# First loads on two queues: queries and keys together on SyncE's, decay table and values on ScalarE's, and eight products of zeros instead of ten

## The chip, the cores and the metric

The kernel runs on one core of a Trainium2 chip. The metric is the device time of one execution in microseconds (us), as the median over several executions. The kernel before takes 665.44 us (median of 6, from 665.19 to 665.92).

## The reference

Two blocks follow each other. The first is a recurrent retention over 4 batches, 8 heads, 768 positions and a head dimension of 64; its output, laid out as 3072 tokens by 512, goes through a two-layer block of width 2048 with a leaky ReLU.

```python
gamma = 1.0 - 2.0 ** (-5.0 - np.arange(H))
scale = 1.0 / np.sqrt(D)
for t in range(S):
    state = gamma[None, :, None, None] * state + einsum('bhd,bhe->bhde', k[:, :, t], v[:, :, t])
    y[:, :, t] = scale * einsum('bhd,bhde->bhe', q[:, :, t], state)
x = y.transpose(0, 2, 1, 3).reshape(3072, 512)
h = x @ w_in                      # 512 x 2048
out = np.maximum(0.01 * h, h) @ w_out   # 2048 x 512
```

## The kernel before

The 768 positions are cut into 6 chunks of 128 (index c), each for 4 batches (b). For one chunk and batch the retention is done in matrix form: `score` multiplies keys by queries (32 small products, L165), `masked` multiplies the result by a triangular mask on VectorE (L187), `decay_v` multiplies the values by a decay per head (L147 on GpSimd, or L151 on ScalarE), `values` multiplies masked scores by values (L210), `reads` adds the part of the running state (L201), `state` and `first_state` form the new state (L225), and `taken` brings the tokens out with their query decay (L255). The tokens of two batches by chunk are then the right-hand side of the two weight layers.

The weights come as 64-bit floats, in 32 pieces of 512 KB. ScalarE (`powers`, L450 to L453) and VectorE (L462, L467, L474) turn each piece into 32-bit floats. The two large layers are done in 2x2 blocks with seven products in place of eight (`seven`, L532); the very first unit alone is done directly (`direct`, L554), in steps that each use one piece.

All this stands in an order written out by hand, and each engine runs its instructions in that order. TensorE's stream at the start is: some products of a cleared tile (`keep_busy`, L744, whose result nobody reads), the scores of chunk 0, batch 0, two small products that spread the decay table over partitions (`tables`, L761 and L763), the scores of batch 1, the `spread` product (L771), the values of batches 0 and 1, the scores of batch 2, one more product of zeros, and then the first step of `direct`.

The first loads are issued from two queues. SyncE's queue (`nc.sync`, SPq in the views) gets queries and keys of batch 0 (512 KB, tile `qk`), values of batch 0 (256 KB, tile `kv`), weight pieces 0 and 1 (tile `raw`), and then queries and keys of batch 2, values of batch 2 and so on. ScalarE's queue (`nc.scalar`, ACTq) gets queries and keys of batch 1, the decay table (24.4 KB, into the tile `rows`, which lies in `t` and is cleared first by GpSimd and VectorE), and values of batch 1. ScalarE then loads its function table and begins to compute only once the decay tables are there. The later loads all come from SyncE's queue; completion semaphores are used in turn, eight of them, so that a later DMA may have to wait for an earlier one's landing.

Of the kernel before, what the change touches and what calls it, by code (L numbers as in the profile page):

```python
# [23 lines left out]
def kernel(  # L24
# [35 lines left out]
    nc = tc.nc  # L60
# [54 lines left out]
    heads = {}  # L115
# [11 lines left out]
            y = flat[:, half : 2 * half].rearrange("p (s h d) -> p s h d", s=2, h=H)  # L127
        heads[c, b] = x, y

    def load_qk(c, b, queue=nc.sync):  # L130
        queue.dma_start(out=heads[c, b][0], in_=qk[c, b])

    def load_v(c, b, queue=nc.sync):
        queue.dma_start(out=heads[c, b][1][:, 1], in_=kv[c, b][:, 1])
# [4 lines left out]
    def load(c, b, place=None):  # L139
        place_for(c, b, place)  # L140
        load_qk(c, b)
        nc.sync.dma_start(out=heads[c, b][1], in_=kv[c, b])
# [15 lines left out]
    def score(c, b):  # L158

        x = heads[c, b][0]  # L160
        ps = scores[c, b] = two_banks(f"ap_{c}_{b}")
        for a in range(HP):
            for u in range(2):
                for j in range(2):
                    nc.tensor.matmul(ps[ts(u, 64), j, a, :], lhsT=x[ts(j, 64), 1, a, ts(u, 64)],  # L165
                                     rhs=x[ts(j, 64), 0, a, :])
# [104 lines left out]
    def ahead(c, b):  # L271


        if c >= NC:
            return
        if b < 2:
            x = work.tile([128, 2, HP, C], FP32, tag="qk", bufs=AHEAD, name=f"qk_{c}_{b}")
        else:
            if b == 2:
                room[c] = new_o(0).rearrange("p i k n -> p (i k n)")  # L280
            x = room[c][:, ds((b - 2) * 2 * HP * C, 2 * HP * C)]
            x = x.rearrange("p (s a t) -> p s a t", s=2, a=HP)
        heads[c, b] = [x, None]
        load_qk(c, b)
# [422 lines left out]
    nothing = t[:, 0, 0, 0:64].bitcast(BF16)  # L707
    half = decay.shape[1] // 2
    load_qk(0, 0)
    load_qk(0, 1, nc.scalar)  # L710
    nc.vector.memset(t[:, 0, 0, 0:64], 0.0)
    nc.gpsimd.memset(rows[:, :half], 0.0)
    nc.vector.memset(rows[:, half:], 0.0)
    nc.scalar.dma_start(out=rows[0:H], in_=decay)
    load_v(0, 0)
    load_v(0, 1, nc.scalar)
    load_piece(0)
    load_piece(1)
# [23 lines left out]
    def keep_busy(n):  # L742
        for _ in range(n):
            nc.tensor.matmul(idle.rearrange("p i (two n) -> p (i two) n", two=2), lhsT=nothing,  # L744
                             rhs=nothing.unsqueeze(1).to_broadcast([128, 4, 128]),
                             start=True, stop=True, skip_group_check=True)
# [9 lines left out]
    def scratch(name, n):  # L756
        return work.tile([128, 2, N], FP32, tag=name, name=f"{name}_x{n}")

    keep_busy(10)
    score(0, 0)  # L760
    nc.tensor.matmul(tables[:, 0, 0:H], lhsT=by_head, rhs=ones, start=True, stop=True,  # L761
                     skip_group_check=True)
# [227 lines left out]
```

## Time and profile before

| what | value |
|---|---|
| median of 6 executions | 665.44 us (665.19 to 665.92) |
| the profiled execution | 665.49 us, of which the span from first to last instruction is 663.4 us |
| mean granted clock of TensorE | 0.999 |
| TensorE busy | 657.6 us (99%) |
| VectorE, ScalarE, GpSimd busy | 371.7, 176.2, 20.5 us |
| TensorE busy in the first 13.7 us | 11.06 us |
| DMA | 48.92 MB in the span; share of the sixteen DMA engines in the first 13.7 us 0.89 |

The profile is that of one execution. Times in its views count from the start of the span. PE is TensorE's products, PEld its loads of the stationary operand, DVE is VectorE, ACT ScalarE, POOL GpSimd, SP SyncE; a line such as "PE ap L165" names the engine, the tile written and the line of the kernel. The chain of waits follows the work back from the last instruction to what released it; a DMA in it stands from its issue to its landing.

### The profile page before, as it was taken

The page shows a single profiled execution, that of the slowest core. Times are in us where ns is not written, and L with a number is a line of the kernel's source. Part 1 is how long each engine was busy: PE and PEld are TensorE (multiplying, and loading weights), DVE is VectorE, ACT ScalarE, POOL GpSimd, SP SyncE. Part 2 cuts the span into 40 slices and gives each one's busy share as a digit, 9 for nine tenths or more (in the row PEclk, how much of TensorE's full clock was granted, in tenths as well). Part 3 has the DMA queues.
Part 4 walks back from the last instruction along what each step waited for, and adds up shares of the span by engine and source line. Part 5 has one row for each costly group of instructions (what it writes and reads, how often), then busy time and mean ns, then how long its engine had stood idle before and what let it go on. Part 6 is the DMA issues. An engine that isn't in the chain of part 4 may idle for free.

```text
span 663.4 us, 10518 instructions
## 1 busy us (share of the span) xinstructions
PE 657.6 (99%) x4537; PEld 574.1 (87%) x4537; DVE 371.7 (56%) x587; ACT 176.2 (27%) x323; POOL 20.5 (3%) x24
## 2 busy tenths in 40 slices
PE   8999999999999999999999999999999999999998
PEld 5888888888888888888888889888888888888886
DVE  5789969889888684243437414527433343431342
ACT  4854555264261002202102211300220210221210
POOL 1000000000000020001001001001000100000000
PEclk9999999999999999999999999999999999999999
DMA  9921422323322650030022003005001001000001
GB/s 339 400 91 33 126 64 77 114 65 107 115 82 77 237 178 1 0 103 26 1 85 107 1 1 127 1 16 176 1 0 33 33 0 48 17 0 1 1 0 63
DMA packets 15757, 48.92 MB, mean 74 GB/s; under 512 B 1752, under 2 KB 2008, under 8 KB 15712
## 3 DMA queue, kind: packets, MB, share of 16 engines
q1 hardware_dynamic: 15408, 47.45, 20.4%
q8 instruction: 35, 0.57, 0.4%
q10 hardware_dynamic: 304, 0.81, 0.3%
q14 instruction: 10, 0.08, 0.0%
HBM read 41.97 MB, written 6.29 MB: 73 GB/s over the span
## 4 chain that ended last, share of the span: by engine, by line
PE 98%; DMA 1%; DVE 0%; issue 0%; DVEq 0%
PE A_o L532 13%; PE B_o L532 13%; PE C_o L532 12%; PE A_h L532 12%; PE B_h L532 12%; PE C_h L532 12%; PE D_o L532 6%; PE D_h L532 6%; PE yp L210 3%; PE d L554 2%; PE ap L301 2%; PE ap L165 2%; PE yp L201 1%; PE sp L225 1%; DMA qk<-in_qk_dram 1%; PE yp L225 0%
## 5 line engine op out<-in xcount | busy, mean ns | idle before, releaser
L532 PE MATMUL A_h<-x,w 128*128 128x256 f32 x368 | 87.7, 381 | 0.0
L532 PEld LDWEIGHTS A_h<-x,w 128*128 128x128 f32 x368 | 69.3, 190 | 9.7 <-issue 0.2
L532 PE MATMUL A_o<-g,w 128*128 128x256 f32 x288 | 68.1, 379 | 0.0
L478 DVE TENSOR_TENSOR m<-m,B_h 128x512 f32<-128x512 f32 x23 | 15.8, 687 | 89.2 <-PE B_h L532 89.2
L532 PEld LDWEIGHTS A_o<-g,w 128*128 128x128 f32 x288 | 54.6, 190 | 7.6 <-issue 0.2
L572 ACT COPY m<-A_h 128x512 f32<-128x512 f32 x23 | 13.5, 585 | 175.8 <-PE A_h L532 155.5
L567 ACT ACTIVATE g<-g 128x512 f32<-128x512 f32 x69 | 42.0, 629 | 66.0 <-DVE g L478 66.0
L478 DVE TENSOR_TENSOR m<-m,B_o 128x512 f32<-128x512 f32 x16 | 11.0, 684 | 64.3 <-PE B_o L532 64.3
L532 PE MATMUL C_h<-t,w 128*128 128x256 f32 x184 | 43.5, 379 | 0.0
L532 PE MATMUL B_h<-x,w 128*128 128x256 f32 x184 | 43.5, 379 | 0.0
L532 PE MATMUL C_h<-x,w 128*128 128x256 f32 x184 | 43.5, 379 | 0.0
L532 PE MATMUL B_h<-t,w 128*128 128x256 f32 x184 | 43.5, 379 | 0.0
L532 PE MATMUL D_h<-t,w 128*128 128x256 f32 x184 | 43.5, 379 | 0.0
L532 PEld LDWEIGHTS C_h<-x,w 128*128 128x128 f32 x184 | 35.0, 190 | 4.8
L532 PEld LDWEIGHTS C_h<-t,w 128*128 128x128 f32 x184 | 35.0, 190 | 4.8
L532 PEld LDWEIGHTS D_h<-t,w 128*128 128x128 f32 x184 | 35.0, 190 | 4.8
L532 PEld LDWEIGHTS B_h<-x,w 128*128 128x128 f32 x184 | 35.0, 190 | 4.8
L532 PEld LDWEIGHTS B_h<-t,w 128*128 128x128 f32 x184 | 35.0, 190 | 4.8
L147 POOL TENSOR_TENSOR kv<-kv,dec 128x512 f32<-128x512 f32 x18 | 19.6, 1089 | 496.5 <-DMA kv<-in_kv_dram 234.8
L481 DVE TENSOR_TENSOR gd<-g,gd 128x512 f32<-128x512 f32 x48 | 33.2, 692 | 1.7
L532 PE MATMUL C_o<-gd,w 128*128 128x256 f32 x144 | 34.0, 379 | 0.0
L532 PE MATMUL B_o<-gd,w 128*128 128x256 f32 x144 | 34.0, 379 | 0.0
(130 smaller groups left out, 1014.8 us busy)
## 6 DMA issues: line engine op xcount, KB each, us to landing
raw<-in_weights_dram SPq DMA_DIRECT2D x31, 512.0 KB, 3.8
kv<-in_kv_dram SPq DMA_DIRECT2D x17, 512.0 KB, 4.8
out_dram<-o SPq DMA_DIRECT2D x23, 256.0 KB, 2.3
qk<-in_qk_dram SPq DMA_DIRECT2D x10, 512.0 KB, 4.5
o<-in_qk_dram SPq DMA_DIRECT2D x8, 512.0 KB, 4.5
in<-in_qk_dram SPq DMA_DIRECT2D x5, 512.0 KB, 8.6
in<-in_kv_dram SPq DMA_DIRECT2D x3, 512.0 KB, 7.8
in<-in_kv_dram SPq DMA_DIRECT2D x4, 256.0 KB, 8.6
```

What stands on the lines that cost most here:

```text
L147: engine.tensor_tensor(out=v, in0=v, in1=gk.unsqueeze(2).to_broadcast([128, H, D]), op=ALU.mult)
L165: nc.tensor.matmul(ps[ts(u, 64), j, a, :], lhsT=x[ts(j, 64), 1, a, ts(u, 64)], rhs=x[ts(j, 64), 0, a, :])
L201: nc.tensor.matmul(ps[ts(i, 64), j, m, :], lhsT=st[b][ts(j, 64), a, :], rhs=x[ts(j, 64), 0, a, :], start=(m == 0), stop=False, skip_group_ ...
L210: nc.tensor.matmul(ps[ts(i, 64), j, m, :], lhsT=y[:, 1, 2 * a + j, :], rhs=am[:, j, a, :], start=(c == 0 and m == 0), stop=True, skip_grou ...
L225: nc.tensor.matmul(sp[ts(j, 64), a, :], lhsT=y[:, 0, 2 * a + j, :], rhs=y[:, 1, 2 * a + j, :], start=start, stop=True, skip_group_check=True)
L301: nc.tensor.matmul(ps[j][ts(u, 64), a, :], lhsT=x[ts(j, 64), 1, a, ts(u, 64)], rhs=x[ts(j, 64), 0, a, :])
L478: nc.vector.tensor_tensor(out=out, in0=a, in1=b, op=ALU.add)
L481: nc.vector.tensor_tensor(out=out, in0=a, in1=b, op=ALU.subtract)
L532: nc.tensor.matmul(half, lhsT=block(w, sa)[:, k, ts(i, 128)], rhs=rhs[:, k, :], start=(first and (i == 0 or split) and n == 0 and k == 0), ...
L554: nc.tensor.matmul(banks[r][:, i, :], lhsT=block(2 * u, r + 2 * kh)[:, k, ts(i, 128)], rhs=x[:, 2 * kh + th, k, :], start=(step == 0 and i ...
L567: nc.scalar.activation(g[:, i], g[:, i], AF.Prelu, alpha=0.01)
L572: nc.scalar.copy(out=got["m1"], in_=ps)
```

## The change

Queries and keys of batches 0 and 1 are both issued from SyncE's queue, one after the other. ScalarE's queue no longer carries queries and keys; it issues the decay table, then the values of batch 0, then those of batch 1. The number of products of zeros at the start goes from ten to eight. All other instructions, their order on each engine and the tiles stay as they are.

```diff
-    def load_qk(c, b, queue=nc.sync):
-        queue.dma_start(out=heads[c, b][0], in_=qk[c, b])
+    def load_qk(c, b):
+        nc.sync.dma_start(out=heads[c, b][0], in_=qk[c, b])
...
     load_qk(0, 0)
-    load_qk(0, 1, nc.scalar)
+    load_qk(0, 1)
     nc.vector.memset(t[:, 0, 0, 0:64], 0.0)
     nc.gpsimd.memset(rows[:, :half], 0.0)
     nc.vector.memset(rows[:, half:], 0.0)
     nc.scalar.dma_start(out=rows[0:H], in_=decay)
-    load_v(0, 0)
+    load_v(0, 0, nc.scalar)
     load_v(0, 1, nc.scalar)
     load_piece(0)
     load_piece(1)
...
-    keep_busy(10)
+    keep_busy(8)
     score(0, 0)
```

## The prediction

> **What bounds the kernel now.** I read the page first, for its shares and the chain that ended last.
>
> ```profile
> PE 657.6 (99%) x4537; PEld 574.1 (87%) x4537; DVE 371.7 (56%) x587; ACT 176.2 (27%) x323; POOL 20.5 (3%) x24
> PE 98%; DMA 1%; DVE 0%; issue 0%; DVEq 0%
> ```
>
> TensorE is busy for 99% of the span and carries 98% of the chain; one per cent of the chain is DMA, at the start. So the change, which touches the first microseconds alone, can only move the moment from which TensorE runs without a gap. The second view is the chain in order of time, cut to the first 30 us (columns: start, duration, what).
>
> ```profile
> 0.80 5.07 DMA qk<-in_qk_dram
> 5.87 0.04 issue
> 5.92 1.10 PE ap L165 x32
> 7.02 0.32 PE tables L761 x2
> 7.34 0.22 PE tables L763 x2
> 7.56 1.03 PE ap L165 x32
> 8.59 1.06 PE spread L771 x2
> 9.65 1.05 PE yp L210 x16
> ...
> 12.60 0.69 DVE w L474
> 13.29 0.04 issue
> 13.33 3.85 PE d L554 x16
> ```
>
> The reader is to see the order: first queries and keys (landed 5.87), scores of batch 0, tables, scores of batch 1, spread, values; then VectorE's work on tokens and on the first weight piece; at 13.33 the first large products. The waits of TensorE after 13 us have a single line, the 0.37 us just ahead of 13.33. What counts is therefore how far 13.33 moves.
>
> The third view is the timeline of the first 5 us (start, duration, engine; SPq and ACTq are the queues of SyncE and ScalarE).
>
> ```profile
> 0.80 0.40 ACTq L131 DMA_DIRECT2D qk<-in_qk_dram  x1
> 0.80 0.38 SPq L131 DMA_DIRECT2D qk<-in_qk_dram  x1
> 1.24 0.42 SPq L134 DMA_DIRECT2D kv<-in_kv_dram  x1
> 1.50 0.52 ACTq L714 DMA_DIRECT2D t<-decay_dram  x1
> 2.05 0.39 ACTq L134 DMA_DIRECT2D kv<-in_kv_dram  x1
> 3.16 0.15 PEld L744 LDWEIGHTS <-t 128*128 128x128 bf16 x1 [0.28 <-issue]
> 3.59 0.61 PEld L744 LDWEIGHTS <-t 128*128 128x128 bf16 x3 [0.28 <-issue]
> ```
>
> The last two lines are the products of zeros: 0.43 us apart until 3.59, then three loads within 0.61 us. The fourth view is the table of stretches (after the stretch: its length, busy time of PE, PEld, DVE, ACT and POOL, then clock, DMA share, GB/s).
>
> ```profile
> 3.00:4.00 1.00, 1.00 (x4) 0.40 (x3) 0.00 (x0) 0.75 (x1) 0.00 (x0) 1.00 0.98 401
> 6.00:8.00 2.00, 2.00 (x56) 1.81 (x60) 0.84 (x1) 0.17 (x1) 0.15 (x1) 1.00 1.03 397
> ```
>
> From 3 us on the sixteen DMA engines are full at about 400 GB/s, so a reordering moves landings against one another, not the total.
>
> **The change part by part.** Everything is set against the profiled execution: span 663.4, time 665.49, so 2.1 us lie around the span; the median 665.44 is 0.05 lower.
>
> *Queries and keys on one queue.* The trace's records of single packets give the price: a 4 KB packet holds an engine 0.159 us, a 2 KB one 0.084; queries and keys of a batch are 8 packets an engine, one batch's values 8 of 2 KB. With both queues filled, their packets alternate. The first packet is slow (0.70 to 1.27 us); on the slowest engine it ends at 3.27. Before, seven more of batch 0 then alternate with six of batch 1 from the other queue: 3.27 + 13 x 0.159 = 5.34, and the landing was at 5.87, some 0.55 later. After, the other queue holds the decay table (one packet of 3 KB, about 0.125) and values: 3.27 + 7 x 0.159 + 0.125 + 5 x 0.084 = 4.93, plus 0.55 gives 5.48. Bounds: 4.93 with nothing between, 5.87 as before. Scores of batch 0 start about 0.4 earlier, near 5.5.
>
> Batch 1 pays for it. Its 8 packets now come after batch 0's, with 8 value packets between: 4.93 + 8 x 0.159 + 8 x 0.084 = 6.87, landing at 7.42, where before it was 6.09 (issued 0.80, landed 5.3 later). Bounds: 6.09, and 7.68 if all the other queue's packets go first (3.27 + 15 x 0.159 + 16 x 0.084 + 0.125 + 0.55). Before, its scores needed it at 7.49 and it had been there for 1.4 us. After, TensorE is ready at about 7.1 (0.4 earlier) and waits for 7.42, so it starts near 7.46: no more than 0.05 us gained. This new wait takes what the old one gave. Queued behind it are spread and values, and VectorE's mask waits for the scores; bounds on this start are 7.1 and 7.72, so -0.4 to +0.25 us.
>
> *Decay table and values.* Decay is issued at 1.50 in both kernels, since it waits for two clearings of its tile that end at 1.40; now it is first on its queue, ahead of 512 KB, and lands near 4 where it was 6.77. The tables need it at about 6.6: no gain, it was there in time. Values of batch 0 are issued at 2.05 instead of 1.24 and land near 5.8 (before 7.09: issue 1.24 and 5.8 to landing), those of batch 1 at 2.45 instead of 2.05 and land near 7.7 (before 9.23: 2.05 and 7.2). GpSimd multiplied batch 1's at 9.30 to 10.34 after a 0.4 us wait; now it starts right behind batch 0's, about 8.9. TensorE needs them at 10.70: this is covered either way, at nothing.
>
> *Queues.* SyncE issues one DMA in place of another, so the weight pieces behind it leave at 1.71 and 2.18 as before. ScalarE still issues three; they end at 2.85 instead of 2.44, and its table load (1.28 us) ends near 4.1. Its first copy starts at 7.60 before, so 3 us of cover hide this. Later issues on SyncE reuse eight completion semaphores in turn: the view of SyncE's waits has 2.5 us for the first DMA. The one behind batch 1's queries moves from 6.26 to about 7.45; its data is wanted by the engines only after 11.4 (batch 2's queries land at 11.37: issued 2.96, 8.4 to landing), and without that cover it would cost up to 1.2 us there.
>
> *Bytes.* Everything that SyncE's queue and the other one carry up to the first weight piece is the same, so this piece still lands at 8.79 (issued 1.71, 7.1 to landing) and the batch 2's queries at 11.37: cost zero, within 0.1 us.
>
> *Two products fewer.* The last two started at 4.10 and 4.32 and nothing but the first scores stands behind them. TensorE stops near 4.3 instead of 4.7, waits till 5.5 instead of 5.9. They cost nothing now, and their absence brings nothing as long as the clock holds, since the data is later.
>
> The sum: -0.05 at the scores of batch 1, 0 elsewhere, carried to 13.33 and the end: 665.49 - 0.05 - 0.05 for the median = 665.4, which I round to 665.35 as the bound on the gain's side is the farther one.
>
> Two rules of the Trainium skill bear on this. The page "DMA: Bandwidth & Descriptors", section "Issuing engines are not separate DMA queues", says that DMAs of all issuing engines interleave on the same sixteen engines and that spreading them saves issue time only; by it alone the change is worth zero. The packets above agree on the sharing, but show that order in a queue moves a landing by 0.4 us or more. The page "TensorE: Matmul & The Clock Gate", section "What's actually happening", speaks against the smaller number of products: the array runs at half rate until about 3.4 us of sustained work; by it eight slow products of 0.427 us, 3.41 us as an estimate, are barely one such stretch.
>
> **The rivals.** *Earlier after all* (0.17): batch 1's data lands before 7.1, for which its packets would need fewer values between them. Then the start moves by 0.4, to 0.6 at most: the batch 2's queries land at 11.37, their scores take 1.03 and the small product behind them 0.2, so 13.33 can't come before 12.7. Time 664.9. For it: the landing of 7.42 is for the slowest engine, whose first packet may be faster another time. Against: the decision needs the last engine.
>
> *Batch 1 late* (0.11): values go through first and 7.68 or later holds. Then +0.25 to +0.5, time 665.8.
>
> *The clock stays low* (0.12), the slower side: place, scores of batch 0 to spread. In the trace the products' pace changed at 3.75, 2.7 us after the first. If in other executions it changes later, ten slow products reach to 1.05 + 4.27 = 5.3 and eight to 4.5, with an idle stretch of a microsecond behind them, and the clock is released only after the scores. Price: twice the time of scores, tables and scores, 1.03 + 0.54 + 1.03 = 2.6 more, less the 0.35 wait for batch 1: about +2.2, time 667.6. It decides (over 1.33 us) when the low clock lasts beyond about 8.8 us in most executions. Against: the six times lie within 0.73 us, and release came while the seventh product ran.
>
> **How the numbers follow.** 0.2% (1.33 us) is about what a measurement of this kernel can tell from no change. The forecast, -0.4 to +0.25, has 0.55; with the two small rivals "same" is 0.83. Slower is the clock, 0.12. Faster by 1.33 us is beyond the 0.6 that the landing at 11.37 allows, so 0.05 is left for what I don't see. The range takes in the two small rivals, 664.9 to 665.9, and the spread of the six times (0.3 to 0.5 around the median): 664.6 to 666.3.
>
> **What would show it.** Right: the wait for the first queries ends near 5.5; a new wait of TensorE or of its loads for queries of some 0.3 us ahead of the second scores, which start at 7.4 to 7.5; the first large product at 13.2 to 13.4; the first piece's landing unchanged. Wrong: second scores at 7.1 (earlier case) or past 7.8 (late), scores that take 2 us instead of 1.03 (clock), the first large product off by over 0.6 us, or a new gap of TensorE after 14 us.

## The result, and the profile after

The changed kernel takes 666.79 us (median of 16), the kernel before 665.44 us. The ratio is 1.0022, with a 95% interval of 1.0014 to 1.003: slower by 1.35 us, just over the 0.2% that can be told from no change, and 0.5 us above the top of the range. The sixteen times fall in two groups: eleven from 666.48 to 667.41 and five from 667.68 to 668.33. The five have a mean granted clock of 0.997, the others 0.999 or 1.0; the profiled execution (667.68 us, span 665.6) is one of the five. So there are two losses to find, one in every execution and one in some. Single executions that took far longer (one of zeros_only below, 1789.18 us, and three of the kernel before) are left out of all counts and ratios.

The page's shares have not moved:

```profile
PE 659.1 (99%) x4535; PEld 575.5 (86%) x4535; DVE 371.2 (56%) x587; ACT 176.5 (27%) x323; POOL 20.1 (3%) x24
PE 98%; DMA 1%; POOL 0%; DVE 0%; ACTq 0%; issue 0%
```

The chain of waits over the first 32 us has changed its beginning (start, duration, what; cut to the part from the issue of the values to the first large product):

```profile
2.49 0.03 issue
2.52 8.30 DMA kv<-in_kv_dram
10.81 0.07 issue
10.88 1.06 POOL kv L147
11.94 0.04 issue
11.98 1.69 PE yp L210 x16
13.66 1.91 PE ap L165 x32
15.58 0.42 PE idle L744
16.00 3.45 PE d L554 x16
```

Before, the chain began with the first queries and ran over scores and VectorE's work to 13.33. Now it begins with the values of batch 1 on ScalarE's queue: issued at 2.52, landed at 10.81, multiplied by GpSimd, and only then used. The large products start at 16.00, 2.67 us later than before; the profiled time is 2.19 us longer, as the first sixteen of them take 3.45 us here and took 3.85 before. The timeline tells what stood ahead of these values:

```profile
0.80 0.86 SPq L131 DMA_DIRECT2D qk<-in_qk_dram  x2
...
1.50 0.58 ACTq L714 DMA_DIRECT2D t<-decay_dram  x1
...
1.71 0.90 SPq L404 DMA_DIRECT2D raw<-in_weights_dram  x2
...
2.11 1.15 ACTq L134 DMA_DIRECT2D kv<-in_kv_dram  x2
...
5.01 1.32 PE L165 MATMUL ap<-qk 64*64 64x128 f32 x32 [0.36 <-DMA qk<-in_qk_dram]
...
6.84 1.10 PE L165 MATMUL ap<-qk 64*64 64x128 f32 x32
...
9.01 1.04 POOL L147 TENSOR_TENSOR kv<-kv,dec 128x512 f32<-128x512 f32 x1 [7.09 <-DMA kv<-in_kv_dram]
...
10.11 1.09 PE L210 MATMUL yp<-am,kv 128*64 128x128 f32 x16 [1.10 <-POOL kv L147]
...
11.98 1.69 PE L210 MATMUL yp<-am,kv 128*64 128x128 f32 x16 [0.78 <-POOL kv L147]
```

The steps of batch 1 in the timeline before, for comparison:

```profile
7.49 1.10 PE L165 MATMUL ap<-qk 64*64 64x128 f32 x32
...
9.30 1.04 POOL L147 TENSOR_TENSOR kv<-kv,dec 128x512 f32<-128x512 f32 x1 [0.41 <-DMA kv<-in_kv_dram]
...
9.58 1.97 PE L210 MATMUL yp<-am,kv 128*64 128x128 f32 x32
```

Both scores do start earlier than before, at 5.01 and 6.84 (5.92 and 7.49 before), without the wait that I expected ahead of the second. The gain is lost at the values' products, which wait 1.10 and 0.78 us for GpSimd. The view of waits up to 17 us puts it on the landing (total, times, longest):

```profile
POOL kv L147 <- DMA kv<-in_kv_dram: 7.9, 2, 7.1
...
PE yp L210 <- POOL kv L147: 1.9, 2, 1.1
```

The second loss is in the table of stretches (length, busy time of PE, PEld, DVE, ACT, POOL, then clock, DMA share, GB/s):

```profile
9.00:10.00 1.00, 0.01 (x1) 0.00 (x0) 1.00 (x2) 0.96 (x2) 0.99 (x1) 1.00 1.02 404
10.00:11.00 1.00, 0.89 (x16) 0.85 (x16) 0.34 (x1) 0.94 (x3) 0.17 (x2) 1.00 1.07 416
11.00:12.00 1.00, 0.22 (x6) 0.02 (x2) 0.68 (x2) 1.00 (x2) 0.93 (x1) 1.00 1.04 410
12.00:14.00 2.00, 2.00 (x24) 1.67 (x28) 0.91 (x3) 1.94 (x6) 0.00 (x0) 0.58 1.04 404
```

TensorE is idle for most of 9 to 10 and of 11 to 12, and then runs at half the clock for 3.4 us (12.33 to 15.74 in the clock's records). That is why the values' products take 1.69 there and the next scores 1.91, where the chain before has 1.05 and 1.03.

### The profile page after: what moved, and what is told of

The parts are those of the page before. It is cut to its first block, busy times and chain, and to the rows that moved or that the text cites. A ratio compares the mean times of both kernels' runs of the same rounds, so it can differ in the third digit from the quotient of the medians.

```text
span 665.6 us, 10513 instructions
## 1 busy us (share of the span) xinstructions
PE 659.1 (99%) x4535; PEld 575.5 (86%) x4535; DVE 371.2 (56%) x587; ACT 176.5 (27%) x323; POOL 20.1 (3%) x24
## 4 chain that ended last, share of the span: by engine, by line
PE 98%; DMA 1%; POOL 0%; DVE 0%; ACTq 0%; issue 0%
PE B_o L532 13%; PE A_o L532 13%; PE C_o L532 12%; PE A_h L532 12%; PE C_h L532 12%; PE B_h L532 12%; PE D_o L532 6%; PE D_h L532 6%; PE yp L210 3%; PE d L554 2%; PE ap L301 2%; PE ap L165 2%; PE yp L201 1%; DMA kv<-in_kv_dram 1%; PE sp L225 1%; PE yp L225 0%
```

## The experiments

From the traces I took the landing of each of the first loads (the last of its completions). Two theories were set against each other. The order theory: a load's data comes in the order in which loads were issued on both queues together, so values issued behind weight pieces come late. The queue theory: ScalarE's queue with its 2 KB packets gets a small share beside SyncE's 4 KB packets, whenever its loads are issued. A third candidate was the missing two products of zeros. Each row is one profiled execution; issue and landing in us:

| kernel | values 0 | values 1 | decay table | piece 0 | first large product | profiled time |
|---|---|---|---|---|---|---|
| before | 1.24, 7.09 | 2.05, 9.23 | 1.50, 6.77 | 1.71, 8.79 | 13.33 | 665.49 |
| changed | 2.11, 8.87 | 2.52, 10.81 | 1.50, 6.20 | 1.71, 8.20 | 16.00 | 667.68 |
| values_first | 0.80, 5.25 | 1.25, 7.79 | 1.80, 8.05 | 1.70, 8.77 | 16.18 | 668.34 |
| qk_only | 1.70, 7.30 | 2.11, 8.88 | 1.50, 5.82 | 2.17, 9.08 | 13.01 | 664.79 |
| pieces_later | 2.11, 7.88 | 2.51, 9.85 | 1.50, 5.98 | 3.15, 9.05 | 13.50 | 665.40 |
| values_on_sync | 1.70, 6.73 | 2.17, 8.07 | 1.50, 6.24 | 2.65, 9.44 | 13.58 | 665.26 |
| v_only | 2.06, 9.20 | 2.48, 11.14 | 1.50, 6.75 | 1.24, 7.69 | 14.80 | 666.87 |

In every row, time less start of the first large product is 651.7 to 652.2: all that happens to the time happens before that product. A landing can differ from one execution to the next: the profiled one of queues_only below, with the loads of the changed kernel, had its values at 9.54 and 11.53, some 0.7 us later than in the table.

**zeros_only: the count of products alone.** The edit is made in the kernel before.

```diff
-    keep_busy(10)
+    keep_busy(8)
```

> The kernel before with eight products of zeros instead of ten, and no other edit. Theory 1 (landings go in the order in which DMAs were issued on both queues together, so the values issued after the weight pieces come late and GpSimd's multiplication holds the first products up): nothing changes, 665.4 us, values of batch 1 landed near 9.2, first large product at 13.3. Rival (the missing two products let TensorE's clock stay low or fall): 666.5 or more, scores that take longer than 1.1 us, mean clock under 0.999.

Median of eleven 668.22, ratio 1.0021 (1.0005 to 1.0038). The times lie in two groups, so the median says little: five from 665.28 to 665.71, six from 668.22 to 668.95. The profile is of the slower group (665.28 against 668.95 is 3.7 us). Its chain:

```profile
5.72 1.98 PE ap L165 x32
7.71 0.52 PE tables L761 x2
8.23 0.42 PE tables L763 x2
8.65 1.92 PE ap L165 x32
10.57 2.00 PE spread L771 x2
...
16.90 3.85 PE d L554 x16
```

and the stretch 8 to 12 of its table:

```profile
8.00:12.00 4.00, 4.00 (x38) 2.65 (x37) 2.44 (x3) 0.17 (x1) 2.04 (x2) 1.00 1.03 408
```

Scores, tables and spread take about twice their time; the records have the clock at half until 13.85. The table's clock column says 1.00 here because it has no record ahead of the release: the durations are what tells. So on the layout before, the two products were not free: without them about half the executions lose 3 us. With ten, 2 of the 34 executions of the kernel before were as long (668.97 and 669.11); neither was profiled. The order theory's expectation of no change failed here, and the rival held.

**queues_only: the queues alone.** The edit is made in the changed kernel.

```diff
-    keep_busy(8)
+    keep_busy(10)
```

> The changed kernel with ten products of zeros as before. Theory 1: as the changed kernel, 666.5 to 667.9, values of batch 0 and 1 landed near 8.9 and 10.8, two waits of TensorE for GpSimd. The first scores may start a little later, which costs nothing. Rival (products of zeros): back to 665.4.

Median 666.71, ratio 1.002 (1.0011 to 1.003): eight times from 666.50 to 666.90 and two, 667.74 and 668.37, with a clock of 0.997. The changed kernel's loss comes from the queues; ten products don't bring it back.

**qk_only: both queries on one queue, and nothing else.** The edit is made in the kernel before.

```diff
-    load_qk(0, 1, nc.scalar)
+    load_qk(0, 1)
```

> The kernel before with one edit: queries and keys of batch 1 issued from SyncE's queue; values of batch 0 stay on SyncE's queue behind them, ScalarE's queue holds decay table and values of batch 1, ten products of zeros. Theory 1: order of issue is queries 0, queries 1, decay, values 0, values 1, piece 0, so values land near 7.3 and 8.2, 665.0 to 665.6. Rival (share of ScalarE's queue): values of batch 1 land near 10.8 and 666.2 or more.

Median 665.03 (664.79 to 666.14), ratio 0.9996 (0.9987 to 1.0005). Values 0 landed at 7.30 as the order theory says, values 1 at 8.88, between the two theories' figures. This half of the change costs nothing.

**v_only: the other half alone.** The edit is made in the kernel before.

```diff
-    load_v(0, 0)
+    load_v(0, 0, nc.scalar)
```

> The other part of the change alone: the kernel before, with the values of batch 0 moved to ScalarE's queue behind the decay table; queries of batch 1 stay first on that queue, ten products of zeros. Order theory: piece 0 is now issued at 1.24 and piece 1 at 1.7, ahead of values 0 (2.05) and values 1 (2.45), so the values land near 9.5 and 10.5 and GpSimd's products hold TensorE up: 666.3 to 668, with some executions at half clock for 3.4 us. If the loss came from both queries on one queue: 665.4.

Median 666.92 (666.64 to 668.13), ratio 1.0026 (1.0017 to 1.0036), two of eleven with a clock of 0.997. The chain again:

```profile
2.48 8.66 DMA kv<-in_kv_dram
...
14.80 3.85 PE d L554 x16
```

Moving 256 KB of values to the other queue is enough for a loss as large as that of the whole change. With it piece 0 is issued at 1.24 and piece 1 at 1.71, before both values. The order of issue is not kept to the letter, though: piece 1 landed at 9.66, behind values 0 (issued at 2.06, landed at 9.20).

**values_first: the same queue, issued earlier.** The edit is made in the changed kernel.

```diff
     load_qk(0, 0)
+    load_v(0, 0, nc.scalar)
     load_qk(0, 1)
+    load_v(0, 1, nc.scalar)
...
     nc.scalar.dma_start(out=rows[0:H], in_=decay)
-    load_v(0, 0, nc.scalar)
-    load_v(0, 1, nc.scalar)
```

> The changed kernel, with ScalarE issuing the values of batch 0 and 1 ahead of the decay table, at about 0.8 and 1.25, so before the weight pieces are issued on the other queue. Queue, packet size and engines of the values stay as in the changed kernel. Theory 1 (order of issue): values land near 5.5 and 7, ahead of the first piece at 8.8; no wait for GpSimd; 664.9 to 665.5. Rival (values on ScalarE's queue with their 2 KB packets get a small share beside 4 KB packets, whatever the order of issue): values land after 8.5 and 10.5 again, 666.4 to 667.9.

The values landed at 5.25 and 7.79, on ScalarE's queue and in 2 KB packets as in the changed kernel: the landings are near the order theory's (it had 5.5 and 7), and against a queue theory in which the values are late whenever they are issued. The time went the other way, 668.43 (median of five, 666.66 to 669.03), ratio 1.0043 (1.0031 to 1.0055). I had not counted what becomes of the decay table, now issued behind piece 0 and, on its own queue, behind both values:

```profile
1.80 6.25 DMA t<-decay_dram
8.05 0.14 issue
8.18 0.36 PE tables L761 x2
8.54 0.22 PE tables L763 x2
8.76 1.77 PE ap L165 x32
```

24.4 KB took until 8.05; its first packet came at 6.80, when nearly all of the values' packets on its own queue had gone (the last ended at 7.11), so this delay does not tell the two orders apart. TensorE waited 1.80 us for it after the first scores, and the clock fell at 8.90, into the second scores.

**pieces_later: the same order on each queue, one issue delayed.** The edit is made in the changed kernel.

```diff
         else:
             raws[n] = place.bitcast(I64)
+        if n == 0:
+            for _ in range(2):
+                nc.gpsimd.memset(raws[n].bitcast(FP32), 0.0)
         nc.sync.dma_start(out=raws[n], in_=weights[n])
```

> The changed kernel, with GpSimd clearing the tile of weight piece 0 twice before SyncE may load it. Queues, their order, packet sizes and bytes stay; only the issue of piece 0 and of what stands behind it on SyncE's queue moves from 1.7 to about 3.5 us, behind the issue of both values on ScalarE's queue (2.1 and 2.5). Order theory: values land near 7.2 and 7.8 instead of 8.9 and 10.8, piece 0 near 9, no wait for GpSimd's product of more than 0.5 us, 664.9 to 665.5: a later load makes the kernel faster. Queue theory (ScalarE's queue gets a small share): values stay near 8.9 and 10.8, 666.4 to 668.

Median 664.99 (664.71 to 665.40), ratio 0.9992 (0.9983 to 1.0001). Against the changed kernel the two useless clearings and a load issued 1.44 us later make 1.8 us less. Piece 0 landed at 9.05, the values at 7.88 and 9.85, earlier by 1.0 each, though not as early as I had said, and TensorE still waited 0.8 us for GpSimd. Half of the values' packets had started by 6.06, ahead of piece 0's (8.06 in the changed kernel); ten of the sixteen parts of values 1 had landed by 7.35, but the last, beside piece 0, at 9.85, behind piece 0 though issued ahead of it. The chain:

```profile
2.51 7.34 DMA kv<-in_kv_dram
...
13.50 3.86 PE d L557 x16
```

(This kernel's lines are three further down.) The values still start the chain, but a microsecond earlier.

**values_on_sync: the values on the other queue, ahead of the pieces.** The edit is made in the changed kernel.

```diff
-    load_v(0, 0, nc.scalar)
-    load_v(0, 1, nc.scalar)
+    load_v(0, 0)
+    load_v(0, 1)
```

> The changed kernel with both values issued on SyncE's queue ahead of the weight pieces; ScalarE issues the decay table alone. Order theory: issue order is queries 0 and 1, decay, values 0, values 1, pieces; values land near 7.3 and 7.9, piece 0 near 9.0, 664.8 to 665.4. A loss that comes from eight products of zeros or from both queries on one queue would stay: 666.5 or more.

Median 665.08 (664.56 to 665.26), ratio 0.9992 (0.9983 to 1.0001). Values at 6.73 and 8.07, piece 0 at 9.44; eight products of zeros and both queries on one queue do no harm here.

**qk_only_8: eight products, with the queries early.** The edit is that of zeros_only, made in qk_only.

> The kernel with both queries on SyncE's queue, values 0 behind them, decay and values 1 on ScalarE's, and eight products of zeros in place of ten. With ten of them on the layout before, the clock was released in time; with eight on that layout (queries landed 5.7) about half the executions took 3 us more with a low clock. Clock theory: what matters is the idle stretch between the products of zeros and the landing of the first queries; here they land near 4.7, the stretch is some 0.3 us, so 664.8 to 665.3 and no execution near 668. If the count of products itself matters: executions near 668 again.

Median 664.99 (664.77 to 665.31), ratio 0.9993 (0.9984 to 1.0002), no execution over 665.31. Its chain has no wait for a load at its head:

```profile
1.05 3.59 PE idle L744 x8
4.64 1.83 PE ap L165 x32
...
7.02 1.03 PE ap L165 x32
...
12.79 3.85 PE d L554 x16
```

The queries (landed 4.54) are there when the products of zeros end. The first scores are slow, since the clock was released at 6.26, and the second are not.

**filled: the waits filled with products.** The edit is made in the changed kernel.

```diff
+    keep_busy(4)
     values(0, 0)
+    keep_busy(3)
     values(0, 1)
```

> The changed kernel with four more products of zeros ahead of the values' products of batch 0 and three ahead of batch 1's, where TensorE waited 1.1 and 0.8 us for GpSimd. They lie in the waits and move nothing. The late values stay, so 666.4 to 667.0; but the executions of the changed kernel near 668, with 3.4 us at half clock from 12.3 on, are gone, as TensorE no longer idles for that long. If the late values alone make those executions, some near 668 remain.

Median 666.78 (666.53 to 667.55), ratio 1.0016 (1.0005 to 1.0028). All eleven executions have a mean clock of 1.0. Two, near 667.5, are above what I gave; their spans, 664.5 us, are like the others', so their excess lies outside the span. None is near 668. The chain still holds the late values and has the first large product at 14.47 instead of 16.00, with full-rate products ahead of it:

```profile
11.99 1.08 PE yp L210 x16
13.08 1.03 PE ap L165 x32
...
14.47 3.86 PE d L554 x16
```

So the late values alone cost some 1.3 us in every execution; the low clock adds about 1.2 to the executions that have it (667.91, the middle of the five, against 666.7).

## Why the prediction was wrong, point by point

**What bounds the kernel** was right: only the moment of the first large product counts, and times follow it within 0.5 us in all kernels of the table.

**Queries on one queue.** The step that failed first is the moment from which ScalarE's queue takes its turns. The sum put batch 0's landing at 5.48 and batch 1's at 7.42; they were 4.97 and 6.33. The alternation of packets itself is in the trace where both queues are moving data. But I let a queue take part within 2 us of its issue. In the changed kernel the decay table, first on an otherwise empty queue and issued at 1.50, has its first packet at 4.66, when SyncE's queue had moved some 850 KB, batch 0's data and two thirds of batch 1's (packet records); the values' first packet is at 6.01, with some 350 KB of piece 0 moved as well. Until 4.66 SyncE's queries had the engines for themselves. So the predicted new wait ahead of the second scores did not come, and they began 0.65 us earlier. The condition of the rival *Earlier after all* (batch 1's data before 7.1) thus came true; qk_only, which has it without the late values, took 665.03, near that rival's 664.9.

**Decay table and values** is the step that decided. I had values landing near 5.8 and 7.7 and wrote that this is covered either way, at nothing; they landed at 8.87 and 10.81. From 6 to 10 us the two queues moved packet for packet, 258 of 4 KB from SyncE's (weight pieces) and 253 of 2 KB from ScalarE's (values), so the values had a third of the bytes. Eight turns at the prediction's prices, 8 x (0.159 + 0.084) = 1.94 us, are just the distance between the two landings. So the values were late because they were issued behind the pieces: they started late, and then ran beside pieces, which the landings of 5.8 and 7.7 left out. With 10.81, GpSimd's 1.06 and TensorE's need at 10.70 before, the sum is 11.98 - 10.70 = 1.28, which would have put the time at 666.7. I gave this term no bounds, though GpSimd's wait of 0.4 us for values 1 was in the timeline. The trace before held the warning: values 1, issued at 2.05 behind piece 0 (1.71), landed at 9.23, behind piece 0 at 8.79, on another queue; its packets ran from 5.68 to 8.59, most of that time beside piece 0's. The alternation as I used it would have had it there by 7.68, the sum that the prediction gives as batch 1's upper bound, since the same packets stood ahead. I did not set the price against that landing.

**Bytes** did not keep to its 0.1 us: piece 0 landed at 8.20 instead of 8.79, most likely since values that the sum had ahead of it now ran beside and behind it; batch 2's queries landed at 11.53 instead of 11.37. **Queues** held in what it concluded: the later issues cost nothing that a run shows, though ScalarE's table load ended at 4.58, not 4.1, and SyncE's later issue stayed at 6.22, not 7.45.

**Two products fewer, and the rival of the low clock.** The rival's mechanism exists and its price was near: 3 us where I had 2.2. But it belongs to the layout before, where queries land at 5.7 to 5.9 (zeros_only). In the change the queries land at 4.97, TensorE idles 0.36 us, and the clock was released at 5.50. The low clock that the change does show comes later, from the idle stretches that the late values make; filled shows no such execution, and 0 of 11 against 5 of 16 makes that likely rather than certain. "They cost nothing" was thus right for the change by luck and wrong for the kernel that I said it of.

**The two rules.** The first gave zero for the change, and it cost 1.35 us: which queue a load is issued from also decides what it runs beside. For sharing, the Trainium skill, page "DMA: Bandwidth & Descriptors", section "Queues, rings and completion order", says that each engine takes turns between the queues that have work, packet by packet. The trace agrees from 6 to 10 us (258 packets against 253). Before that, a queue with an issued load got no packet for 3.2 us (1.50 to 4.66); whether the engines had work from it by then, no view shows. The Trainium skill, page "TensorE: Matmul & The Clock Gate", section "What's actually happening", has the clock released by sustained work of about 3.4 us and taken back after an idle window as long; here it fell after 1.9 us of idle time in the 3.4 us before 12.33, and in the slower zeros_only execution it stayed at half through 8.1 us of work without a gap (5.72 to 13.85). The measurement decides.

**Open.** The runs show that values issued behind weight pieces of the other queue land late and cost the time, and that issued ahead of the pieces, on either queue, they do not land late (values_first, values_on_sync) or less so (pieces_later). They do not show what in the chip holds a later load back, how much of the delay is the late start and how much the sharing, nor why the last parts of values 1 in pieces_later trail so far behind the others. Which executions fall to the low clock was not controlled in any run.

qk_only_8, values_on_sync and pieces_later are all faster than both kernels in the median, by 0.3 to 0.4 us against before; each interval reaches past 1, so against the kernel before this is a hint and no more. Against the changed kernel qk_only_8 makes 1.8 us less, with no execution of its eleven within a microsecond of the changed kernel's fastest.

## What to carry to other kernels

When loads saturate the DMA engines, write down all loads of all queues in the order of their issue: in these runs a load moved to an empty queue but issued later was a later load, and what moved up in the old queue passed it or ran beside it. Where two queues run beside each other, count packets and not bytes: a queue of 2 KB packets beside one of 4 KB had a third of the bytes. The list gives the order of most landings here, not of all. Before pricing a reordering with a model of sharing, set the model against every landing that the trace before has, above all the one that is not first on its queue. Filler products for the clock are to be judged by the time to the next landing, and waits of TensorE near the start can cost a second time through the clock (here waits of 1.10 and 0.78 us, and 1.2 us more in 5 of 16 executions).

## What the runs showed of the hardware that I had not expected

A load of 24.4 KB, first on its queue, landed 4.7 us after its issue when a megabyte had been issued before it on the other queue (changed kernel); in values_first, with 512 KB of values ahead of it on its own queue as well, 6.25 us after. Two queues that both move data alternated by packets and not by bytes: 258 packets of 4 KB against 253 of 2 KB in 4 us. In the slower zeros_only execution TensorE was busy without a gap from 5.72 with scores of 64x64 tiles, small tables and the spread, and the clock stayed at half until 13.85. Whether small tiles count for less toward the release was not tried.
